# Windowed attention ahead of two MLPs: old and new scores merged by mask into 128 columns before the exponential

## The chip, the cores and the metric

One core of one Trainium2 chip. The metric is device time in microseconds (us), the median of three runs. Engines: PE multiplies matrices (PEld loads its stationary side), DVE is VectorE, ACT is ScalarE, POOL is GpSimd, SP issues most DMAs.

## What is computed

Attention over `q`, `k`, `v` of shape (2, 8, 768, 64) (batch, heads, positions, width), in which a position sees itself, the 127 positions before it, and the first four positions (the sinks); then two MLPs over the 1536 tokens of 512, of width 2048:

```
scores = scale * q @ k^T
keep = (pos_k < 4) | ((rel >= 0) & (rel < 128))          # rel = pos_q - pos_k
a = softmax(where(keep, scores, -1e9));  x = a @ v
x -> (x @ w_in), g = h if h >= 1, 0 if h <= -1, else (h + 1)^2 / 4;  x = g @ w_out
x -> (x @ w2_in), g = h if h > 0, else exp(h) - 1;                   out = g @ w2_out
```

All is float32; the weights arrive as 64-bit numbers and are converted on the chip.

## The kernel before

*Attention* (class `Attn`). 768 positions are six blocks of 128. A segment is two blocks of one batch: six segments. A job is one pair of heads of a segment, four jobs a segment, 24 in all. A job goes through these steps:

- **T** (`st_T`, line 456): k and q are transposed on PE (line 466, four transposes) and copied to `qkT` (line 470, on DVE in the front, on ACT later). POOL keeps the last block of k for the next segment and copies the four sink keys behind each block (lines 474 to 481).
- **S0, S1** (`st_S`, line 484), one for each block: for each of the two heads one matmul (line 506) of 128 queries against 260 columns: 128 old keys (the block before), 4 sinks, 128 new keys. The first block of a batch has no old keys and 132 columns. DVE adds the mask, scales and takes the maximum (line 510), ACT takes the exponential and its sum (line 512), POOL copies the sink columns (line 515).
- **X** (`st_X`, line 531): the probabilities are transposed on PE (line 539), 128 columns at a time: two for a block with old keys, so eight for a job, six in the first segment of a batch; ACT copies them to `pt` (line 541), one copy for each head.
- **V** (`st_V`, line 544): v times `pt` (line 564), the two heads in two 64-column halves of the array; DVE copies the result to `xb` (line 567).
- After four jobs the **sink stage** (`st_sink`, line 569) adds the sinks' part, divides by the sums and writes the token tiles `xh`, `xl` for the MLPs. `vsink` (line 353) sets up the sink values; `load_vsink` (line 345) loads them by two DMAs from ACT's queue.

*The MLPs* (class `Moe`). 96 items: two MLPs, three token tiles of 512, 16 pieces of the width. An item is 12 matmuls of 512 columns in `gemm1` (line 171) and 12 in `gemm2` (line 210), which runs two items later; each product is made of three matmuls on split numbers. The weights of an MLP are converted once, with its first token tile (lines 138 to 145, ACT and DVE), and split for each item (`wsplit`, line 158 on ACT, line 160 on DVE in the first 16 items and on POOL later).

*Order.* `stages` (line 403) is a generator which gives one step at a time; `ahead` (line 415) and `FIRST` say how far T, S0 and S1 of a job run ahead of its V. The first two segments run before the MLPs (lines 764 to 774), with PE's order as it is written; the accumulator banks that the MLPs do not yet need serve as spares (`spare`), eight in all. Then `between` (line 779) draws steps from the generator at each of the four stops of an item, with `PULLS` steps for each stop: 1.0 in the first token tile, 0.8 in the second; there the attention has two banks. The DMAs of the front are issued in program order (lines 764 to 770, and `load` in `stages`).

## Time and profile before

| | us |
|---|---|
| median of three runs | 661.48 (661.33 to 661.95) |
| the profiled execution | 662.93 |
| its span, first to last instruction | 661.2 |
| PE busy | 638.8 (97%) |
| ACT busy | 450.6 (68%) |
| DVE busy | 376.2 (57%) |
| POOL busy | 267.8 (40%) |

The span lies inside the execution's time; 1.7 us lie around it. Shares over the whole span hide that the kernel has parts with different limits: the first product matmul (line 171) starts at 58.0 us, the attention is over before 266.5 us, and the rest is products. So the rows are cut by these times, and the first part of the products once more at 152.8 us, where the conversion of the first weights ends. Busy time of an engine is the time in which at least one of its instructions ran; neighbouring instructions overlap a little, so that means of single instructions add up to more than that. An entry "x4" counts records; a matmul on float32 leaves two records, a transpose one.

### The profile page before, as it was taken

What the parts mean: (1) busy time and instruction counts of PE and PEld (TensorE: products, weight loads), DVE (VectorE), ACT (ScalarE), POOL (GpSimd) and SP (SyncE); (2) the same over time, 40 slices, a digit from 0 to 9 for tenths busy, and PEclk for the clock granted to TensorE, in tenths of its full rate; (3) what the DMA queues carried; (4) which work ended last, traced back from release to release, by engine and by line L of the source; (5) the groups of instructions that cost most, each with busy time, mean ns of one, the idle gap of its engine ahead of it and who ended that gap; (6) DMA issues with size and microseconds to landing.
All of it is one profiled execution on the core that took longest, in us unless ns stands there. A gap on an engine that the chain in (4) does not pass through costs nothing.

```text
span 661.2 us, 9257 instructions
## 1 busy us (share of the span) xinstructions
PE 638.8 (97%) x3090; PEld 500.5 (76%) x3090; DVE 376.2 (57%) x742; ACT 450.6 (68%) x913; POOL 267.8 (40%) x310
## 2 busy tenths in 40 slices
PE   5899999999999999999999999999999999999995
PEld 2666767766777767888878888888888888888884
DVE  2899989999435244224987878777432222322221
ACT  2998998997666666557768878776655555555542
POOL 4320113112125334443645655554544444444441
PEclk8998999999999999999999999999999999999999
DMA  6577454764200000000433332321010000100001
GB/s 172 126 186 203 126 170 135 207 198 143 56 13 13 13 0 1 1 0 1 159 118 105 99 105 90 109 93 50 0 64 1 0 1 0 64 0 1 1 0 69
DMA packets 66922, 47.91 MB, mean 72 GB/s; under 512 B 44848, under 2 KB 61232, under 8 KB 66864
## 3 DMA queue, kind: packets, MB, share of 16 engines
q1 hardware_dynamic: 65552, 46.94, 24.6%
q8 instruction: 26, 0.43, 0.3%
q10 hardware_dynamic: 1312, 0.28, 0.2%
q14 instruction: 32, 0.26, 0.1%
HBM read 44.06 MB, written 3.15 MB: 71 GB/s over the span
## 4 chain that ended last, share of the span: by engine, by line
PE 81%; DVE 7%; issue 4%; ACT 4%; DMA 2%; POOL 1%; POOLq 0%; SPq 0%; DVEq 0%; ACTq 0%
PE h L171 36%; PE y L210 35%; PE S L506 4%; PE ops L564 3%; PE tps L539 2%; DVE ca L143 2%; PE qkps L466 1%; DVE F L145 1%; DVE ca L142 1%; DVE wl L160 1%; ACT pt L541 1%; DMA st<-in_moe_w_in_dram 1%; DVE P L510 1%; ACT P L512 1%; PE y L267 1%
## 5 line engine op out<-in xcount | busy, mean ns | idle before, releaser
L160 POOL TENSOR_TENSOR wl<-F,wh 128x512 fp32r<-128x512 f32 x160 | 219.6, 1380 | 229.6 <-ACT wh L158 216.9
L158 ACT CAST wh<-F 128x512 fp32r<-128x512 f32 x192 | 117.5, 618 | 97.1 <-PE h L171 89.4
L171 PE MATMUL h<-xh,wh 128*128 128x512 f32 x384 | 154.3, 402 | 0.5 <-DVE g L180 0.5
L171 PE MATMUL h<-xh,wl 128*128 128x512 f32 x384 | 150.5, 392 | 0.0
L171 PE MATMUL h<-xl,wh 128*128 128x512 f32 x384 | 150.5, 392 | 0.0
L187 ACT CAST gh<-g 128x512 fp32r<-128x512 f32 x96 | 59.7, 621 | 62.1 <-DVE g L184 36.2
L188 DVE TENSOR_TENSOR gl<-g,gh 128x512 fp32r<-128x512 f32 x96 | 68.3, 712 | 49.0 <-ACT gh L187 48.7
L184 DVE SCALAR_TENSOR_TENSOR g<-g,h 128x512 f32<-128x512 f32 x48 | 33.0, 687 | 110.9 <-ACT g L183 110.9
L171 PEld LDWEIGHTS h<-xh,wh 128*128 128x128 f32 x384 | 72.4, 189 | 20.6 <-issue 5.3
L171 PEld LDWEIGHTS h<-xh,wl 128*128 128x128 f32 x384 | 72.3, 188 | 15.3
L171 PEld LDWEIGHTS h<-xl,wh 128*128 128x128 f32 x384 | 72.7, 189 | 14.2 <-DVE xl L608 0.4
L210 PE MATMUL y<-gh,wh 128*128 128x512 f32 x192 | 78.4, 408 | 0.0
L210 PE MATMUL y<-gh,wl 128*128 128x512 f32 x192 | 75.2, 391 | 0.0
L210 PE MATMUL y<-gl,wh 128*128 128x512 f32 x192 | 74.9, 390 | 0.0
L145 DVE CUSTOM_DVE_ANT_0 F<-ca,F 128x1024 uint16<-128x1024 uint16 x64 | 71.5, 1119 | 4.5 <-DVE ca L143 1.8
L210 PE MATMUL y<-wh,gh 128*128 128x512 f32 x184 | 71.6, 389 | 0.0
L210 PE MATMUL y<-wl,gh 128*128 128x512 f32 x184 | 71.6, 389 | 0.0
L210 PE MATMUL y<-wh,gl 128*128 128x512 f32 x184 | 71.6, 389 | 0.0
L180 DVE SCALAR_TENSOR_TENSOR g<-h,g 128x512 f32<-128x512 f32 x48 | 33.0, 687 | 45.2 <-ACT g L179 45.1
L512 ACT ACTIVATE P<-P,nb 128x260 f32<-128x260 f32 (+1 forms) x96 | 46.6, 491 | 15.5 <-DVE nb L510 13.4
L515 POOL COPY psn<-P 128x8 f32<-128x8 f32 x48 | 13.0, 271 | 89.8 <-ACT P L512 81.9
L510 DVE CUSTOM_DVE_ANT_0 P<-S,mask 128x260 f32<-128x260 f32 (+1 forms) x96 | 34.8, 401 | 24.1 <-PE S L506 23.5
(105 smaller groups left out, 912.3 us busy)
## 6 DMA issues: line engine op xcount, KB each, us to landing
st<-in_moe_w_in_dram SPq DMA_DIRECT2D x32, 512.0 KB, 3.9
st<-in_moe_w_out_dram SPq DMA_DIRECT2D x32, 512.0 KB, 3.8
kn<-in_k_dram SPq DMA_DIRECT2D x48, 64.0 KB, 2.3
vn<-in_v_dram SPq DMA_DIRECT2D x32, 96.0 KB, 2.4
out_dram<-o SPq DMA_DIRECT2D x12, 256.0 KB, 2.1
qn<-in_q_dram SPq DMA_DIRECT2D x44, 64.0 KB, 2.4
vn<-in_v_dram SPq DMA_DIRECT2D x16, 64.0 KB, 2.1
qn<-in_q_dram ACTq DMA_DIRECT2D x4, 64.0 KB, 3.0
```

The lines of the kernel that those rows point to most:

```text
L145: nc.vector.tensor_tensor(out=r, in0=ai, in1=r, op=ALU.add)
L158: nc.scalar.copy(hi, src)
L160: (nc.vector if i < self.KF else nc.gpsimd).tensor_tensor(out=lo, in0=src, in1=f32(hi), op=ALU.subtract)
L171: nc.tensor.matmul(h, lhsT=w[:, k * 128:(k + 1) * 128], rhs=x[:, k, c0:c0 + n], start=(k == 0 and p == 0), stop=(k == self.KD - 1 and p == 2))
L180: nc.vector.scalar_tensor_tensor(out=g, in0=h, scalar=1.0, in1=g, op0=ALU.max, op1=ALU.min)
L184: nc.vector.scalar_tensor_tensor(out=g, in0=g, scalar=-1.0, in1=h, op0=ALU.add, op1=ALU.max)
L187: ac = nc.scalar.copy(gh, g)
L188: dv = nc.vector.tensor_tensor(out=gl, in0=g, in1=f32(gh), op=ALU.subtract)
L210: nc.tensor.matmul(self.y[c], lhsT=a, rhs=b, start=(first and p == 0), stop=(last and p == 2))
L506: nc.tensor.matmul(S[h], lhsT=qT[hs, n, :], rhs=kT[hs].rearrange("p j k -> p (j k)")[:, j0 * KW:j0 * KW + W], start=True, stop=True)
L510: dv = nc.vector.tensor_tensor_reduce(out=o, in0=S[h], in1=self.mask[ty], op0=ALU.add, op1=ALU.min, scale=-self.scale, scalar=3.0e38, accu ...
L512: ac = nc.scalar.activation(o, o, AF.Exp, bias=nb[:, n, h:h + 1], scale=-1.0, accum_out=sm[:, n, 2 * pr + h:2 * pr + h + 1])
```

## The change

- Of each block's 128 columns, a query needs either the old or the new key: column c is new for queries from c on, and old for those before. The scores of a block are made in 64x64 tiles, in such places that for half of the columns the wanted score is where it should be; where a 64x64 square holds both kinds, DVE copies one over the other by a mask (`copy_predicated`, two for a head). So 128 columns and 4 sinks are left for the maximum and the exponential, instead of 260 columns.
- S0 and S1 become one step S, with both blocks of a pair in one bank for each head.
- X transposes four tiles instead of eight and ACT makes one copy; POOL separates old and new by two `affine_select` of 512 elements.
- The copy to `qkT` is on ACT throughout, and that to `xb` too.
- Order: V of a job is drawn one job later, T, S and V have new places, `PULLS` is (0.7, 0.7, 1.0), `FIRST` 8; loads of k and q run four jobs ahead instead of three; in the front POOL too follows the written order.
- The sink values' selectors (`sink_sets`) are made ahead of the front; the rest of `vsink` stays in the first sink stage; `load_vsink` is issued on SP, after the loads of v of job 0.

```diff
-PULLS = (1.0, 0.8, 1.0)
+PULLS = (0.7, 0.7, 1.0)
 LAG = 2
-FIRST = 9
+FIRST = 8
 NSINK = 4
 BLK = 128
 KW = BLK + NSINK
-WP = KW + BLK
+HB = BLK // 2
+BW = KW + HB + NSINK
...
-        self.ld_p = pool("ld", 3)
+        self.ld_p = pool("ld", 4)
+        self.v_p = pool("v", 3)
         self.qk_p = pool("qk", 2)
-        self.p_p = pool("p", 4)
+        self.p_p = pool("p", 3)
...
+        pick = const.tile([128, HB], F32, tag="pickf", name="pickf")
+        nc.gpsimd.memset(pick, 1.0)
+        for c, op, sg in ((0, ALU.is_ge, 1), (1, ALU.is_gt, -1)):
+            r = pick[c * HB:(c + 1) * HB]
+            nc.gpsimd.affine_select(out=r, in_=r, pattern=[[-sg, HB]], compare_op=op, fill=0.0, base=0, channel_multiplier=sg)
...
-            self.nc.scalar.dma_start(out=raw[:, 0, :], in_=self.v[b, :, 0:NSINK, :])
+            self.nc.sync.dma_start(out=raw[:, 0, :], in_=self.v[b, :, 0:NSINK, :])
...
+    def sink_sets(self):
...
-        ahead = (("T", 2), ("S0", 1), ("X", 0), ("S1", 1), ("V", 0))
-        todo = {p: [] for p in range(-2, len(jobs))}
+        ahead = (("S", 1), ("T", 2), ("V", -1), ("X", 0))
+        todo = {p: [] for p in range(-3, len(jobs) + 1)}
         for j in range(len(jobs)):
             for i, (what, d) in enumerate(ahead):
-                todo[max(j - d - (j < FIRST and d > 0), -2)].append((j, i, what))
-        sink = None
-        for p in range(-2, len(jobs)):
-
-            order = "XT01V".index if self.spare else "T0X1V".index
-            for j, _, what in sorted(todo[p], key=lambda x: (order(x[2][-1]), x[0])):
+                todo[max(j - d - (j < FIRST and d > 0), -3)].append((j, i, what))
+        sink, ready = {}, []
+        for p in range(-3, len(jobs) + 1):
+
+            order = ("XTVS" if p < FIRST else "VXTS").index if self.spare else "STVX".index
+            for j, _, what in sorted(todo[p], key=lambda x: (order(x[2]), x[0])):
                 seg, pr = jobs[j]
                 st = state[seg]
-                if what == "V" and sink:
-                    yield from sink[0]
-                    yield sink[1]
-                    sink = None
                 if what == "T":
                     self.st_T(seg, pr, st)
-                    load("k", j + 3)
-                    load("q", j + 3)
-                elif what == "S0":
-                    self.st_S(seg, pr, st, 0)
-                elif what == "S1":
-                    self.st_S(seg, pr, st, 1)
+                    load("k", j + 4)
+                    load("q", j + 4)
+                elif what == "S":
+                    self.st_S(seg, pr, st)
+                    ready.append((seg, pr, st))
                 elif what == "X":
                     self.st_X(seg, pr, st)
+                    while ready:
+                        self.sums(*ready.pop(0))
                 else:
                     self.st_V(seg, pr, st)
                     load("v", j + 2)
                 yield None
-            if p >= 0 and jobs[p][1] == np_ - 1:
+                if what == "V" and pr == np_ - 1:
+                    yield from sink[seg]
+                    yield seg
+            if 0 <= p < len(jobs) and jobs[p][1] == np_ - 1:
                 seg = jobs[p][0]
-                sink = self.st_sink(seg, state[seg]), seg
-                if self.spare and p + 1 < len(jobs):
-
-                    yield next(sink[0])
-                else:
-                    yield from sink[0]
-                    yield seg
-                    sink = None
+                sink[seg] = self.st_sink(seg, state[seg])
+                yield next(sink[seg])
 
...
-        late = self.spare and (seg, pr) not in self.jobs[:2]
-        (nc.vector.tensor_copy if late else nc.scalar.copy)(T[:, 1:, 0:BLK], bank)
+        nc.scalar.copy(T[:, 1:, 0:BLK], bank)
...
+    def st_S(self, seg, pr, st):
+
         nc, D, nq = self.nc, self.D, self.nq
         b, q0 = seg[0], seg[1]
+        qT, T = st["qk", pr]
+        Tk = T.rearrange("p j k -> p (j k)")
+        if "sm" not in st:
+            st["sm"] = self.s_p.tile([128, nq, self.H], F32, tag="sm", name="sm")
+            st["ps"] = self.s_p.tile([128, nq, self.H * (NSINK + 2)], F32, tag="psn", name="psn")
+        nb = self.s_p.tile([128, nq, 2], F32, tag="nb", name="nb")
+        P = st["P", pr] = self.p_p.tile([128, nq, 2, KW], F32, tag="P", name="P")
+        S = [self.bank([128, 512], "S") for _ in range(2)]
+        lead = HB + NSINK
+        for n in range(nq):
+            u = lead + n * BW
+            for h in range(2):
+                hs = slice(h * D, (h + 1) * D)
+                for c in range(2):
+                    o, r = (u - c * lead, n * KW + c * HB) if q0 + n else (u, KW)
+                    N = (KW + (HB, lead)[c]) if q0 + n else KW
+                    nc.tensor.matmul(S[h][c * HB:(c + 1) * HB, o:o + N], lhsT=qT[hs, n, c * HB:(c + 1) * HB],
+                                     rhs=Tk[hs, r:r + N], start=True, stop=True, skip_group_check=True)
+        n0 = 0 if q0 else 1
         for h in range(2):
+            a = S[h][:, lead:lead + nq * BW].rearrange("p (n c) -> p n c", c=BW)
+            lo = S[h][:, 0:nq * BW].rearrange("p (n c) -> p n c", c=BW)
+            for c, to, data in ((0, a[:, :, 0:HB], a[:, :, KW:KW + HB]), (1, a[:, :, HB:BLK], lo[:, :, 0:HB])):
+                r = slice(c * HB, (c + 1) * HB)
+                nc.vector.copy_predicated(to[r, n0:], self.pick[r].unsqueeze(1).to_broadcast([HB, nq - n0, HB]), data[r, n0:])
+            for n in range(nq):
+                o = P[:, n, h, :]
+                dv = nc.vector.tensor_tensor_reduce(out=o, in0=a[:, n, 0:KW], in1=self.mask[min(q0 + n, 2)], op0=ALU.add, op1=ALU.min,
+                                                    scale=-self.scale, scalar=3.0e38, accum_out=nb[:, n, h:h + 1])
+                ac = nc.scalar.activation(o, o, AF.Exp, bias=nb[:, n, h:h + 1], scale=-1.0,
+                                          accum_out=st["sm"][:, n, 2 * pr + h:2 * pr + h + 1])
...
+    def sums(self, seg, pr, st):
+        nc = self.nc
+        P = st["P", pr]
+        sinks = st["ps"][:, :, 2 * pr * NSINK:2 * (pr + 1) * NSINK]
+        nc.gpsimd.tensor_copy(sinks.rearrange("p n (h s) -> p n h s", h=2), P[:, :, :, BLK:KW])
+    def st_X(self, seg, pr, st):
+        nc, nq = self.nc, self.nq
+        P = st["P", pr]
+        bank = self.bank([128, 2 * nq, 128], "tps")
         for h in range(2):
+            for n in range(nq):
+                nc.tensor.transpose(bank[:, h * nq + n, :], P[:, n, h, 0:BLK], self.idn)
+        t = st["pt", pr] = self.pt_p.tile([128, 4 * nq, 128], F32, tag="pt", name="pt")
+        t2 = t.rearrange("p (a two) q -> p a two q", two=2)
+        old, new = t2[:, :, 0, :], t2[:, :, 1, :]
+        nc.scalar.copy(new, bank)
+        for o, op, sg in ((old, ALU.is_gt, 1), (new, ALU.is_ge, -1)):
+            nc.gpsimd.affine_select(out=o, in_=new, pattern=[[0, 2 * nq], [-sg, 128]], compare_op=op, fill=0.0, base=0,
+                                    channel_multiplier=sg)
...
+        nc.scalar.copy(st["xb"][:, pr, :], bank)
 
...
-        for what, j in (("k", 1), ("k", 2), ("q", 2), ("v", 0)):
+        for what, j in (("k", 1), ("k", 2), ("q", 2), ("k", 3), ("q", 3), ("v", 0)):
             attn.load(what, *attn.jobs[j])
-        with tc.manual_schedule(engines={mybir.EngineType.PE}):
-            go(n=1)
+        attn.load_vsink()
+        attn.sink_sets()
+        with tc.manual_schedule(engines={mybir.EngineType.PE, mybir.EngineType.Pool}):
             moe.load(1)
             attn.load("v", *attn.jobs[1])
             moe.load(3)
-            go(n=19)
-        flag = windowed(tc, const, prm)
-        with tc.manual_schedule(engines={mybir.EngineType.PE}):
+            go(n=18)
+            flag = windowed(tc, const, prm)
             go(upto=need[0])
```

## Rows read from the trace of the kernel before

**Rows 1.** Stretch, length, busy PE, PEld, DVE, ACT, POOL, granted clock, DMA share, GB/s.

```profile
18.00:58.00 40.00, 35.21 (x281) 25.64 (x279) 36.81 (x129) 39.17 (x118) 9.99 (x42) 1.00 0.66 164
58.00:152.80 94.80, 93.82 (x478) 67.66 (x478) 87.52 (x203) 86.12 (x192) 15.90 (x38) 0.98 0.60 173
152.80:266.50 113.70, 112.53 (x600) 82.88 (x599) 55.45 (x130) 74.73 (x166) 41.67 (x53) 1.00 0.10 26
266.50:649.60 383.10, 382.61 (x1687) 315.98 (x1685) 188.89 (x249) 244.69 (x426) 190.82 (x139) 1.00 0.14 46
```

**Rows 2.** Chain of waits, 58 to 190 us: start us, length us, what.

```profile
166.95 0.44 PE qkps L466 x4
167.39 1.40 PE y L210 x6
168.78 0.64 PE S L506 x4
169.42 1.59 PE y L210 x6
171.01 0.87 PE tps L539 x8
...
175.49 1.02 PE ops L564 x12
```

**Rows 3.** The same chain over the whole span, where products run alone.

```profile
280.25 2.72 PE y L210 x12
```

**Rows 4.** Timeline, 5 to 15.5 us: start, length, engine, line, operation [idle <-releaser].

```profile
5.40 2.05 ACTq L350 DMA_DIRECT2D vraw<-in_v_dram  x2
...
7.49 1.28 ACT L741 ACT_TABLE_LOAD   x1 [7.49 <-DMA qn<-in_q_dram]
...
11.64 0.61 POOL L368 CAST one<-oneh 112x512 fp32r<-112x512 f32 x1
...
12.57 1.03 POOL L385 TENSOR_TENSOR vs<-vpart,sel 96x512 fp32r<-96x512 f32 x1
13.03 0.96 SPq L398 DMA_DIRECT2D kn<-in_k_dram  x2
...
13.79 1.68 PE L506 MATMUL S<-qkT 64*128 64x132 f32 x8 [6.36 <-POOL qkT L481]
...
14.97 0.41 ACT L512 ACTIVATE P<-P,nb 128x132 f32<-128x132 f32 x1 [5.03 <-DVE nb L510]
```

**Rows 5.** Groups by line and shape, whole span: busy us, mean ns | idle before.

```profile
L512 ACT ACTIVATE P<-P,nb 128x260 f32<-128x260 f32 x80 | 40.3, 509 | 9.6 <-DVE nb L510 7.5 <-POOL qkT L481 1.6
...
L510 DVE CUSTOM_DVE_ANT_0 P<-S,mask 128x260 f32<-128x260 f32 x80 | 30.9, 423 | 17.1 <-PE S L506 16.6 <-POOL qkT L481 0.3
...
L541 ACT COPY pt<-tps 128x512 f32<-128x512 f32 x32 | 17.4, 579 | 2.5 <-PE tps L539 2.4
...
L567 DVE COPY xb<-ops 128x256 f32<-128x256 f32 x24 | 10.1, 420 | 12.3 <-PE ops L564 12.1
...
L512 ACT ACTIVATE P<-P,nb 128x132 f32<-128x132 f32 x16 | 6.3, 399 | 5.9 <-DVE nb L510 5.8
...
L510 DVE CUSTOM_DVE_ANT_0 P<-S,mask 128x132 f32<-128x132 f32 x16 | 4.0, 289 | 7.1 <-PE S L506 6.9
...
L332 DVE SCALAR_TENSOR_TENSOR mask<-rel,prm,mask 128x128 f32<-128x128 f32 x2 | 0.7, 344 | 0.0
...
L340 DVE COPY mask<-mask 128x128 f32<-128x128 f32 x1 | 0.2, 218 | 0.0
```

**Rows 6.** Timeline, 53 to 59 us.

```profile
54.13 0.52 ACT L512 ACTIVATE P<-P,nb 128x260 f32<-128x260 f32 x1
...
55.13 0.51 ACT L512 ACTIVATE P<-P,nb 128x260 f32<-128x260 f32 x1
```

**Rows 7.** Line 145 by stretch: minimum/median/maximum ns, first and last start.

```profile
L145 DVE CUSTOM_DVE_ANT_0 F<-ca,F x26: 675/686/1357, 57.4 to 149.8; 128x1024 uint16<-128x1024 uint16 x26
...
L145 DVE CUSTOM_DVE_ANT_0 F<-ca,F x30: 682/1622/1705, 314.0 to 454.9; 128x1024 uint16<-128x1024 uint16 x30
```

More of the change, by code (lines that the diff above doesn't have):

```diff
@@ new lines, in masks @@
+        self.pick = const.tile([128, HB], I32, tag="pick", name="pick")
+        nc.gpsimd.tensor_copy(self.pick, pick)
+        nc.vector.tensor_scalar(out=neg, in0=rel, scalar1=0.0, scalar2=None, op0=ALU.is_lt)
+        nc.vector.scalar_tensor_tensor(out=ring, in0=neg, scalar=float(BLK), in1=rel, op0=ALU.mult, op1=ALU.add)
+        nc.vector.scalar_tensor_tensor(out=far, in0=neg, scalar=1.0e6, in1=rel, op0=ALU.mult, op1=ALU.add)
+        m0, m1, m2 = self.mask = [const.tile([128, KW], F32, tag=f"mask{ty}", name=f"mask{ty}") for ty in range(3)]
@@ L351, in load_vsink @@
             self.vraw.append(raw)
+    def sink_sets(self):
+        nc, const, H, D = self.nc, self.const, self.H, self.D
+        R = H * NSINK
+        L = 3 * R + 2 * H
+        self.one = const.tile([L, H, D], F32R, tag="one", name="one")
+        one = const.tile([L, H], F32, tag="oneh", name="oneh")
+        nc.gpsimd.memset(one, 0.0)
+        for j in range(2):
+            nc.gpsimd.affine_select(out=one[3 * R:], in_=one[3 * R:], pattern=[[-1, H]],
+                                    compare_op=ALU.not_equal, fill=1.0, base=-j * H, channel_multiplier=1)
+        nc.gpsimd.tensor_copy(self.one, one.unsqueeze(2).to_broadcast([L, H, D]))
+        self.sel = const.tile([3 * R, H], F32, tag="sel", name="sel")
+        nc.gpsimd.memset(self.sel, 1.0)
+        for g in range(3):
+            s = self.sel[g * R:(g + 1) * R]
+            nc.gpsimd.affine_select(out=s, in_=s, pattern=[[-NSINK, H]], compare_op=ALU.is_ge, fill=0.0,
+                                    base=0, channel_multiplier=1)
+            nc.gpsimd.affine_select(out=s, in_=s, pattern=[[NSINK, H]], compare_op=ALU.is_ge, fill=0.0,
+                                    base=NSINK - 1, channel_multiplier=-1)
@@ L481, in st_T @@
         nc.gpsimd.tensor_copy(kT[:, :, BLK:], self.sk[pr].to_broadcast([128, nq + lead, NSINK]))
[L482 to L484 removed]
+        if q0 + nq < self.S // BLK:
+            nc.gpsimd.tensor_copy(self.kept[pr], T[:, nq, 0:BLK])
+        st["qk", pr] = qT, T
+    def st_S(self, seg, pr, st):
         nc, D, nq = self.nc, self.D, self.nq
         b, q0 = seg[0], seg[1]
[L487 to L517 removed]
@@ L519, in chunks @@
-    def chunks(self, q0):
-        out = []
-        for n in range(self.nq):
-            qb = q0 + n
-            if qb == 0:
-                out.append((n, 0, 0))
-            else:
-                out.append((n, 0, qb - 1))
-                out.append((n, KW, qb))
-        return out
-    def st_X(self, seg, pr, st):
-        nc, D, nq = self.nc, self.D, self.nq
-        b, q0 = seg[0], seg[1]
-        P = st.pop(("P", pr))[0]
-        ch = self.chunks(q0)
-        for h in range(2):
-            bank = self.bank([128, len(ch), 128], "tps")
-            for i, (n, o, kb) in enumerate(ch):
-                nc.tensor.transpose(bank[:, i, :], P[n][:, h, o:o + 128], self.idn)
-            t = self.pt_p.tile([128, len(ch), 128], F32, tag="pt", name="pt")
-            nc.scalar.copy(t, bank)
-            st["pt", pr, h] = t
+        qT, T = st["qk", pr]
@@ L548, in st_V @@
         vn = self.nat.pop(("v", seg, pr))
-        ch = self.chunks(q0)
-        runs = []
-        for i, (n, o, kb) in enumerate(ch):
-            if runs and runs[-1][0] == kb:
-                runs[-1][2] += 1
-            else:
-                runs.append([kb, i, 1])
+        first = 1 if q0 == 0 else 0
+        runs = [(q0 - 1, 0, 1)] * (1 - first) + [(q0 + n, 2 * n + 1, 2 if n + 1 < nq else 1) for n in range(nq)]
         if "xb" not in st:
```

115 lines of the change are left out of this document (32 added, 83 removed).

## Prediction

> **What bounds the kernel now.** I read the busy time by stretch first [rows 1]. From 266.5 us on, PE is busy for 382.61 of 383.10 us with the two products alone: no attention is left there, so the change can gain nothing in it. From 58.0 to 266.5 the products and attention share PE, which is full in both stretches (93.82 of 94.8 us, 112.53 of 113.7). In the first of them DVE (87.52 us) and ACT (86.12 us) are nearly full as well, because the weights are converted there; in the second they have room. Before 58.0 it is another matter: from 18 to 58 us ACT is busy 39.17 of 40 us, DVE 36.81, PE 35.21. So the front is bound by ACT, with DVE close behind, and the middle by PE.
>
> Next the chain of waits in a steady piece of the middle [rows 2]. It gives the price of an attention step on PE: its own piece, plus what the six product matmuls behind it take above 1.36 us, their pace when nothing lies between (2.72 for twelve, [rows 3]). A T costs 0.44 + 0.03 = 0.47 us, an S step of one block 0.64 + 0.23 = 0.87, an X of eight transposes 0.87 + 0.03 = 0.90, a V 1.02 + 0.23 = 1.25. A job (one pair of heads, two blocks) has two S steps: 4.36 us. By the order that the code yields, 22 groups of twelve product matmuls and about 7.3 jobs lie in the first stretch of the middle, and some 15 jobs in all after 58 us; 15 x 4.36 = 65 us agrees with what is left of 208.5 us after 50 groups x 2.72 = 136 us (72.5, with four sink stages and small waits in it).
>
> Last the start of the front [rows 4]. PE's first scores wait until 13.79 us, 6.36 us of it for POOL, which copies the sink keys into qkT only behind the set-up of the sink values (up to the 1.03 us product at 12.57). That set-up waited for the vraw DMAs, whose issue holds ACT's queue for 2.05 us from 5.40, so that ACT's table load stands at 7.49 and its first exponential at 14.97.
>
> **The change, part by part.** *Scores.* The steps S0 and S1 become one. A transpose's piece (four of 128 columns in 0.44 us, [rows 2]) gives 0.11 us for 128 columns in one pass; a step's four records (two heads, two passes, 260 columns) would take 0.89 us one after another and take 0.64 with their entry, so two row halves already run side by side; V's twelve records (16 units of 128 columns, 1.76 us in a row) take 1.02, so two column halves do too. Four 64x64 tiles at once are in no row. If both kinds compose, a block costs two passes of 200 columns = 0.34 us instead of 0.45, and entering and leaving (0.87 - 0.45 = 0.42) is paid once for two blocks: 0.42 + 0.69 = 1.11 us instead of 1.74, a gain of 0.63. If the column halves queue, it is 0.42 + 1.38 = 1.80, a loss of 0.06. I take the first, as V's row shows the column side at the same width of 64.
>
> *Transposes.* Four instead of eight (six in the first segment of a batch): 0.45 us off, or 0.22. V keeps its columns.
>
> *PE in the middle.* 15 jobs x 0.63 = 9.4; 11 x 0.45 + 4 x 0.22 = 5.8; together 15.2 us. The new order leaves one S, one T and one X more to the middle (scores of jobs 0 to 8 in front instead of 0 to 9): 1.11 + 0.47 + 0.45 = 2.0 back. Left: 13 us.
>
> *DVE in the middle.* A job's four evacuations go from 260 to 132 columns, 423 to 289 ns [rows 5]: -0.54 us; the xb copy (420 ns) goes to ACT; four predicated copies of 64 partitions x 128 elements come. The trace has none. Below, the plain 128-element copy (218 ns); above, the dearest 128-element instruction (344 ns); I take 0.29, the row for 132 columns read from PSUM with a second operand. Net +0.2 us a job. But the pulls fall from 1.0 to 0.7 a call, with 20 steps in a segment instead of 24: 6.2 jobs instead of 7.3 lie in the first stretch, so DVE there stays near 86 us of work while PE's falls from 94 to about 84. DVE takes over as the bound of that stretch, and two nearly full engines wait for each other. In addition both banks go to one S step, and the T behind it waits until DVE has emptied the first (two copies, two evacuations: about 1.1 us, against 1.4 us of products in between). For all this I take 3 us off, bounds 0 and 7. PE in the middle: -10 us, between -6 and -13.
>
> *POOL.* Two selects of 512 elements a job: between 0.61 (the cast of 512 elements) and 1.03 us each (the product of two tensors, [rows 4]), so 1.2 to 2.1 us a job, against about 3 us a job of ACT in front. V is moved a job behind X, so this is hidden; if POOL's hand-written order fails to keep up, V waits, and that is in the rivals.
>
> *Front, start.* The sink values' set-up moves to the first sink stage; only the selectors, which wait for nothing, stay ahead. The vraw DMAs go to SP. The first scores then wait for ACT's copy of qkT: about 2 us earlier without the DMA issues, then a few tenths of POOL's sink copies. First exponential near 9.7 instead of 14.97: -5 us, -4 if ACT gains nothing. SP pays: k and q of job 4 are issued behind four more DMAs and 1.5 MB of weights, at 0.48 us apiece [rows 4], and land near 18 us, some 1.5 us after ACT wants them.
>
> *Front, ACT's work.* The first and the third exponential of a job start 1.00 us apart, accumulators included [rows 6]; at 132 columns they are 110 ns shorter [rows 5], so 0.39 each instead of 0.50. One pt copy of two falls away (579 ns in its row; with the overlap of 0.1 that neighbours on ACT show, an estimate of 0.48; 0.38 for the three-chunk copies of a first segment), one T copy of the same size comes from DVE, and an xb copy of half of it (estimate 0.30). Front, before: scores 10 x 2.0, pt 10 x 0.48 + 8 x 0.38, T 3 x 0.48 = 29.3. After: 9 x 1.56 + 8 x 0.48 + 10 x 0.48 + 8 x 0.30 = 25.1. So -4 us. At the end the last V now stands behind a select and nothing of X or S is left to fill ACT: +1.5.
>
> *Sum.* Front -5 + 1.5 - 4 + 1.5 = -6 (between -2 and -10); middle -10; the stretch after 266.5 unchanged. -16 us on a span of 661.2, or of 662.93 for the profiled execution with what lies around it: 646.9. The median of the runs, 661.48, lies 1.45 below that execution, so I predict 645.5.
>
> **The rivals.**
> A, *DVE sets the middle.* With conversions, 128-column selects and bank waits the first stretch hardly shrinks (94.8 to about 93), and the gain of the middle is 5: 651. For it: 87.52 of 94.8 us [rows 1], and a conversion instruction of DVE which takes 686 ns there but 1622 where POOL splits weights all the time [rows 7]; 12 selects that each held one up by 0.65 would add 8 us to DVE. Against it: POOL is busy only 15.90 us in that stretch now. The Trainium skill's "TensorEngine Tiling (Array Packing)", section PSUM Bottleneck, says that tiling speeds TensorE but not the emptying of PSUM, which may become the bound; by that rule A is the outcome, 651, and the trace bears it out for that stretch alone. "SBUF — State Buffer" of the Trainium skill, section Who interferes with whom, says that DVE and GpSimd share one port pair as an exclusive lock; rows 7 agree for this instruction.
>
> B, *the four tiles don't run side by side.* The scores' gain of 9.4 us becomes a loss of 0.9; partly hidden where DVE binds: 655.
>
> C, *slower: two banks and one DVE queue.* PE takes its instructions in order. If DVE reaches the score evacuations only behind a whole conversion and a split (four instructions of up to 0.69 us, the length of L145 in [rows 7]; an estimate of 2.5), a bank comes free 2.5 + 1.1 us after the scores, against 1.4 to 2.8 us of products; T and the next S then each stand for about a microsecond. Ten jobs in the converting stretch x 2 us = 20, against 16 + 3 gained: 662.5. It decides from 1.8 us a job. Against it: V, X and T need only one bank each now.
>
> D, *the front gains all of its 10 us and nothing waits in the middle*: 638.
>
> **How the numbers follow.** Forecast 0.64 (639 to 652), A 0.15, B 0.06, C 0.09, D 0.06. A difference under 0.2% (1.3 us) can't be told from no change here. Faster: forecast, A, B, D and little of C = 0.89; slower 0.07; same 0.04. The range must take in D's edge and A and B: 637 to 656; C is left out.
>
> **What would show it.** Right: the first L171 matmul near 52 us instead of 58; the first exponential near 10; S as one piece of about 0.9 us with eight records a block starting together; tps pieces of 0.44 us; product groups at 1.36 to 1.6 us with attention over before 262 us. A would show as DVE busy over 95% up to the last conversion, with PE waiting for it; B as S pieces of 1.6 us; C as PE waits on the mask evacuation ahead of T and S of over 1 us each. I would be wrong in the front if a late k or q, or POOL's selects ahead of V, stop ACT there.

## The result: slower, and where the time went

The changed kernel takes 668.36 us (median; 667.26 to 669.76) where the kernel before takes 661.5: ratio 1.0104, 95% interval 1.0084 to 1.0123. The forecast was 645.5, the range 637 to 656. The traces are of single executions, 668.36 us after and 662.93 before; their spans are 666.2 and 661.2 us.

The stretches of [rows 1], now of the kernel after (same columns):

```profile
18.00:58.00 40.00, 28.62 (x257) 19.67 (x258) 30.62 (x114) 29.58 (x91) 21.67 (x47) 0.85 0.66 165
58.00:152.80 94.80, 88.07 (x503) 63.80 (x500) 89.61 (x213) 81.26 (x187) 25.86 (x42) 0.98 0.54 153
152.80:266.50 113.70, 110.59 (x660) 82.15 (x659) 63.58 (x170) 76.23 (x183) 53.84 (x68) 1.00 0.18 49
266.50:649.60 383.10, 382.86 (x1671) 310.26 (x1670) 190.46 (x251) 243.08 (x426) 191.50 (x141) 1.00 0.15 46
```

Three things are to be seen. In the front no engine is full any more: ACT fell from 39.17 to 29.58 of 40 us, PE from 35.21 to 28.62, and PE's granted clock is 0.85. In the second row PE has lost work (93.82 to 88.07) and DVE is now the fuller engine. In the last row PE is as full as before but has done 1671 matmuls instead of 1687.

That last row is the surprise. The chain of waits between 400 and 420 us, where products run alone (start, length, what):

```profile
404.51 2.80 PE h L172 x12
407.31 2.74 PE y L211 x12
410.05 2.80 PE h L172 x12
412.85 2.74 PE y L211 x12
```

Before, twelve matmuls of either product took 2.72 us. [rows 3] shows it for y; the chain of the kernel before between 400 and 420 us shows it for h:

```profile
409.12 2.72 PE h L171 x12
```

The same instructions at the same granted clock of 1.00 now take 2.80 and 2.74: one item (twelve h, twelve y) 5.54 us instead of 5.44, one h matmul 233.3 ns instead of 226.7.

Landmarks read from PE's own records (starts of matmuls; an item is 24 product matmuls, 96 items in all):

| | before | after |
|---|---|---|
| first product | 58.0 | 59.4 |
| item 16 | 189.4 | 183.2 |
| item 32 | 299.1 | 298.6 |
| last matmul | 654.6 | 659.9 |

The front lost 1.4 us (forecast: a gain of 6), items 0 to 31 gained 1.9 (forecast 10, and some of that is eaten by the slower pace), and 64 items without any attention lost 5.9 (forecast 0). Together +5.3, from starts that are not rounded.

The front's start went nearly as forecast. PE's timeline of the kernel after (start, length, instruction, idle time before it):

```profile
8.30 0.79 PE L509 MATMUL S<-qkT 64*64 64x132 f32 x16 [0.77 <-POOL qkT L484]
...
21.23 0.66 PE L472 MATMUL qkps<-idn,kn 128*128 128x128 f32 x2 [6.84 <-DMA kn<-in_k_dram]
...
23.75 1.39 PE L509 MATMUL S<-qkT 64*64 64x132 f32 x16
...
27.62 0.91 PE L509 MATMUL S<-qkT 64*64 64x196 f32 x16
```

ACT's first exponential, from the same stretch:

```profile
10.39 0.41 ACT L522 ACTIVATE P<-P,nb 128x132 f32<-128x132 f32 x1
```

Scores start at 8.30 instead of 13.79 and the first exponential at 10.39 instead of 14.97 [rows 4]. Then PE stands for 6.84 us for k of job 4. SP's queue in the same stretch shows what stood ahead of it:

```profile
12.08 0.44 SPq L107 DMA_DIRECT2D st<-in_moe_w_in_dram  x1
12.57 1.01 SPq L403 DMA_DIRECT2D vn<-in_v_dram  x2
13.63 0.47 SPq L110 DMA_DIRECT2D st<-in_moe_w_out_dram  x1
14.14 0.43 SPq L107 DMA_DIRECT2D st<-in_moe_w_in_dram  x1
14.70 0.94 SPq L410 DMA_DIRECT2D kn<-in_k_dram  x2
```

The k load was issued right behind three weight loads of 512 KB each, and from 14 to 22 us the DMA engines are busy 0.99 of the time, at 272 GB/s. In the kernel before the same three loads were issued from 8.37 to 12.51 us, while PE stood 6.36 us for POOL [rows 4], and its trace has no wait of PE for a load between 8 us and the first product.

### The profile page after: what moved, and what is told of

Same layout as the page of the kernel before. It is cut to its first block, busy times and chain, and to the rows that moved or that the text cites. A ratio compares the mean times of both kernels' runs of the same rounds, so it can differ in the third digit from the quotient of the medians.

```text
span 666.2 us, 9583 instructions
## 1 busy us (share of the span) xinstructions
PE 631.7 (95%) x3202; PEld 489.3 (73%) x3202; DVE 386.8 (58%) x805; ACT 444.2 (67%) x922; POOL 303.7 (46%) x337
## 4 chain that ended last, share of the span: by engine, by line
PE 75%; DVE 8%; ACT 6%; DMA 4%; issue 3%; POOL 1%; SPq 1%; POOLq 0%; ACTq 0%; DVEq 0%
PE h L172 34%; PE y L211 33%; PE ops L565 2%; PE S L509 2%; DMA st<-in_moe_w_in_dram 2%; DVE ca L144 2%; DVE F L146 2%; ACT P L522 1%; PE qkps L472 1%; PE tps L541 1%; ACT F L140 1%; ACT ca L139 1%; DMA kn<-in_k_dram 1%; DVE ca L143 1%; PE y L268 1%
## 5 line engine op out<-in xcount | busy, mean ns | idle before, releaser
L172 PE MATMUL h<-xl,wh 128*128 128x512 f32 x384 | 152.3, 397 | 0.9 <-POOL xl L609 0.9
L189 DVE TENSOR_TENSOR gl<-g,gh 128x512 fp32r<-128x512 f32 x96 | 72.7, 758 | 51.5 <-ACT gh L188 51.1
L146 DVE CUSTOM_DVE_ANT_0 F<-ca,F 128x1024 uint16<-128x1024 uint16 x64 | 74.3, 1164 | 4.3 <-DVE ca L144 1.8
L547 POOL TENSOR_SCALAR_AFFINE_SELECT pt<-pt 128x512 f32<-128x512 f32 x48 | 35.7, 744 | 32.5 <-ACT pt L545 30.9
L139 ACT ACTIVATE ca<-st 128x512 f32<-128x512 f32 x64 | 43.1, 674 | 7.4 <-DVE F L146 3.4
L144 DVE SCALAR_TENSOR_TENSOR ca<-st,ca 128x512 int32<-128x512 int32 x64 | 47.3, 742 | 1.1
```

The source lines that it names most:

```text
L139: nc.scalar.activation(a, w1.bitcast(F32), AF.Copy, scale=2.0 ** -112)
L144: nc.vector.scalar_tensor_tensor(out=ai, in0=w1, scalar=-0x80000000, in1=ai, op0=ALU.bitwise_and, op1=ALU.bitwise_or)
L146: nc.vector.tensor_tensor(out=r, in0=ai, in1=r, op=ALU.add)
L172: nc.tensor.matmul(h, lhsT=w[:, k * 128:(k + 1) * 128], rhs=x[:, k, c0:c0 + n], start=(k == 0 and p == 0), stop=(k == self.KD - 1 and p == 2))
L189: dv = nc.vector.tensor_tensor(out=gl, in0=g, in1=f32(gh), op=ALU.subtract)
L547: nc.gpsimd.affine_select(out=o, in_=new, pattern=[[0, 2 * nq], [-sg, 128]], compare_op=op, fill=0.0, base=0, channel_multiplier=sg)
```

## Experiments: the products' pace

The same program text computes the products in both kernels. What differs is where their tiles stand in SBUF: the change alters the sizes of the attention tiles, and the x tiles and MLP tiles (weights, split weights, g) are allocated around them. Before, x begins at byte 27040 of a partition and the split weights (wh0) at 192672; after, at 26528 and 196320. The experiments move tiles and touch nothing else. Edits are on the kernel named first.

**e1, before, x and MLP tiles where after has them.**

```
-            raw = self.const.tile([R, 1, self.D], F32, tag=f"vraw{b}", ...)
+            raw = self.vr_p.tile([R, 1, self.D], F32, tag=f"vraw{b}", ...)
+        self.vr_p = pool("vr", 1)      # behind a_s
+        self.pad = pool("pad", 1).tile([128, 912], F32, tag="pad", name="pad")
```

> The kernel before, with the token tiles and all tiles of the MLPs at the very SBUF addresses that they have in the changed kernel (x 512 bytes lower, the MLP's tiles 3648 bytes higher); no instruction differs. Theory P (the changed kernel's slower products, 5.54 us an item instead of 5.44, come from where the tiles lie): the items of the last stretch go to 5.54 us, and the time rises by 96 x 0.10 = about 9.5 us, to 671. Theory Q (they come from something else in the change): 661.5, items at 5.44.

668.30 us, ratio 1.0105 (1.0088 to 1.0122), an item 5.54 us: the kernel before, with nothing but addresses changed, is as slow as the kernel after. Theory P's pace came, its 671 did not: the 64 items of pure products got 5.9 us longer, items 0 to 31 no longer (240.4 us, before 241.1).

**e2 and e3, one group of tiles each**: only the vr_p line (x 512 bytes lower), or only the pad (MLP tiles 3648 bytes higher).

> The kernel before, with the token tiles alone 512 bytes lower, where the changed kernel has them; MLP tiles as before. If the place of the moving token tiles is what matters: gemm1's matmuls at 233 ns, gemm2's at 227, some 7.5 us more (669). If the place of the MLP tiles is what matters: 661.5.

> The kernel before, with the MLP's tiles alone 3648 bytes higher, where the changed kernel has them; token tiles as before. If the place of the weights and of g matters: gemm1 and gemm2 both slower, 668 to 671. If the token tiles' place matters: 661.5 to 663.

e2: 661.45, 5.44 us an item. e3: 669.09, ratio 1.0124 (1.0104 to 1.0144), 5.54. So it is the MLP tiles' place, and the next three ask how finely it counts, and whether against x.

**e5, e6, e7: 64 bytes.** A tile of [128, 16] float32 ahead of the MLP tiles (e5 in after, e6 in before), or ahead of x, so that all move (e7, in before).

> The kernel after with one unused tile of 64 bytes a partition behind the attention pools, so that every MLP tile stands 64 bytes higher: at 32 modulo 128, as in the kernel before (before: 110752 and so on, 160 modulo 2048; after: 114400, 1760 modulo 2048, which is 96 modulo 128); nothing else is changed. Theory P1 (the products' pace hangs on where the MLP tiles stand within 128 bytes): an item of pure products falls from 5.54 to 5.44 us, the time from 668.4 to 661 (659 to 663). Theory P2 (it hangs on the place within a larger unit, or on how high the tiles stand): 5.54 us and 668 as after.

> The kernel before with the same 64-byte tile: MLP tiles at 96 modulo 128, everything else where it was. P1: an item of pure products goes from 5.44 to 5.54 us, 661.5 to 668.5 (667 to 670). P2: 5.44 us and 661.5.

> The kernel before with a 64-byte tile ahead of the x tiles, so that x, the attention tiles and the MLP tiles all stand 64 bytes higher, at 96 modulo 128 (x at 27104). P1 with the place itself counting: 5.54 us an item and 668.5. P1 with the place of the weights against x counting (both were at 32 modulo 128 before; here both are at 96): h matmuls at 226.7 ns as before, and 661.5 to 663 in all. P2: 661.5.

e5: 667.10, 5.53 us an item, a miss for P1; its chain of waits:

```profile
403.69 2.79 PE h L172 x12
406.49 2.73 PE y L211 x12
```

e6: 669.45, ratio 1.0115 (1.0098 to 1.0132), 5.54: 64 bytes cost 7.5 us. e7: 662.03, 5.44: the same 64 bytes cost nothing when x moves along. The chain of waits of e6:

```profile
408.65 2.74 PE y L210 x12
411.39 2.80 PE h L171 x12
```

And that of e7:

```profile
407.96 2.72 PE h L171 x12
410.68 2.72 PE y L210 x12
```

The distance between x, which the h matmul streams, and wh0, which it loads as weights, orders all these runs:

| kernel | x | wh0 | distance | remainder to 256 | item, us |
|---|---|---|---|---|---|
| before | 27040 | 192672 | 165632 | 0 | 5.44 |
| e2 | 26528 | 192672 | 166144 | 0 | 5.44 |
| e7 | 27104 | 192736 | 165632 | 0 | 5.44 |
| e6 | 27040 | 192736 | 165696 | 64 | 5.54 |
| e3 | 27040 | 196320 | 169280 | 64 | 5.54 |
| after, e1 | 26528 | 196320 | 169792 | 64 | 5.54 |
| e5 | 26528 | 196384 | 169856 | 128 | 5.53 |

The MLP tiles moved as one group in every run, so the table alone does not tell the weights from the other MLP tiles, which ACT, DVE and POOL read and write meanwhile. The trace of the kernel after narrows it. From 320 to 655 us it has 30 places where an h matmul follows another while ACT, DVE and POOL all stand (in 29 of them no DMA moves bytes either), and each of these steps takes 233 ns, like the others. One of them lies between the end of a POOL instruction (560.51 + 1.29) and the start of one on ACT (562.29):

```profile
560.51 1.29 POOL L161 TENSOR_TENSOR wl<-F,wh 128x512 fp32r<-128x512 f32 x1 [1.76 <-ACT wh L159]
561.80 0.39 PE L172 MATMUL h<-xl,wh 128*128 128x512 f32 x1
562.04 0.39 PE L172 MATMUL h<-xh,wl 128*128 128x512 f32 x1
562.29 0.62 ACT L159 CAST wh<-F 128x512 fp32r<-128x512 f32 x1 [1.86 <-PE h L172]
```

So the slower pace needs no other engine at work. What h itself reads in SBUF is x and the split weights.

**e9, the test of that rule on the kernel after**: the two 16-byte nb tiles (64 bytes with their alignment) go ahead of x, so that the distance becomes 169728, which leaves nothing over 256.

```
+    Attn.nb_p = ctx.enter_context(tc.tile_pool(name="nb", bufs=2))   # ahead of xp
-        nb = self.s_p.tile([128, nq, 2], F32, tag="nb", name="nb")
+        nb = self.nb_p.tile([128, nq, 2], F32, tag="nb", name="nb")
```

> The kernel after with the two 16-byte nb tiles ahead of the x tiles instead of behind the other attention tiles: x stands 64 bytes higher, the MLP tiles stay where the kernel after has them, and the distance from x to the split weights is 169728 bytes instead of 169792. Theory R (the distance from the moving x tile to the split weights decides: no remainder to 256 bytes in the three kernels with 5.44 us an item, 64 or 128 in the five with 5.53 to 5.54): an item of pure products takes 5.44 us, the time falls from 668.4 by 7 to 9 us to 660 (659 to 661.5), so the kernel after is faster than before by 0 to 0.4%. Rival H (how high the tiles stand, or the place of x alone): 5.54 us and 668.

660.52 us, ratio 1.0005 (0.9981 to 1.0029). Its chain:

```profile
408.68 2.72 PE y L211 x12
411.40 2.72 PE h L172 x12
```

The pace is back, 7.8 us with it, and what is left of the change is a difference from before that can't be told from none. Against the kernel before, e9's first product is 0.6 us later, and items 0 to 31 take 237.4 us instead of 241.1; the profiled execution (659.52) is one of the shortest of e9's ten (659.46 to 667.04).

## Experiments: the front

Five kernels, all made from after with its slow pace, move the three weight loads or free POOL's order.

**e4 and e11, the loads later in SP's queue.** In after, the front begins with load(1), v of job 1, load(3), and then 18 steps.

```
e4:   +go(n=2)   moe.load(1)   attn.load("v", ...)   moe.load(3)   go(n=16)
e11:   attn.load("v", ...)   go(n=6)   moe.load(1)   go(n=4)   moe.load(3)   go(n=8)
```

> The changed kernel with two steps (T of jobs 0 and 1) drawn ahead of the first three weight loads, so that k and q of jobs 4 and 5 are issued before 1.5 MB of weights. Theory L (the front lost its gain because k of job 4 lands only at 21.1 us): PE's wait of 6.8 us for it shrinks to under 2, the first product comes at 55 us instead of 59.4, and the time falls by about 4 us, to 664. Theory M (the front is bound by the order of POOL and the waits between engines): the load comes earlier, but the first product stays within 1 us of 59.4.

> The kernel after with v of job 1 issued first, and the three first weight loads (1.5 MB) behind the sixth and the tenth step of the front instead of ahead of the first. Theory D: without these 1.5 MB at 12 to 22 us the k, q and v loads land when they are wanted, PE's waits for DMA in the front (6.8 for k, 1.6 for v) go, and the first product comes at 53 to 56 us, the time at 662 to 665. Rival L (a chain of latencies through PE, DVE, ACT and POOL sets the pace once the loads are there): first product at 58 to 60, 667 to 669.

e4: 667.15, first product at 59.9: theory M's outcome, since PE waits for k of job 4 no more and for no other load by more than 1.6 us (v), and still the products begin no earlier. e11: 667.49, first product at 60.0: rival L's outcome, though here a load is late again, v instead of k. SP's queue in e11:

```profile
25.37 0.47 SPq L110 DMA_DIRECT2D st<-in_moe_w_out_dram  x1
25.88 0.43 SPq L107 DMA_DIRECT2D st<-in_moe_w_in_dram  x1
26.36 1.37 SPq L403 DMA_DIRECT2D vn<-in_v_dram  x2
```

And PE's timeline in e11:

```profile
31.73 1.75 PE L565 MATMUL ops<-pt,vn 128*64 128x256 f32 x8 [6.24 <-DMA vn<-in_v_dram]
```

In after and in e11 the wait of 6 to 7 us hits the load that is issued right behind the weights. e4 shows that this wait is not what the front's length hangs on alone. One term that the waits do not show is PE's clock: the granted clock from 18 to 58 us is 1.00 in before [rows 1], 0.85 in after, 0.81 in e11 and 0.74 in e4 (before has its low stretch earlier, 0.50 from 12 to 18 us). In e4 PE was busy for 4.24 of the 8 us from 14 to 22 us; then the granted clock is 0.50, the level of 1.2 GHz, from 22 to 30 us. It is low again from 39 to 46 us (0.53), and a step S takes 1.61 us there, one of the same size behind it 0.91:

```profile
41.17 1.61 PE L509 MATMUL S<-qkT 64*64 64x196 f32 x16
45.64 0.91 PE L509 MATMUL S<-qkT 64*64 64x196 f32 x16
```

How much of the front the clock costs, against the engines' waits for each other, no run separates.

**e13, the loads on ACT's queue; e16, behind steps 14 and 16.**

```
e13:  +eng = nc.scalar if self.n_ld <= 3 else nc.sync      # in Moe.load, for both DMAs
e16:   attn.load("v", ...)   go(n=14)   moe.load(1)   go(n=2)   moe.load(3)   go(n=2)
```

> The kernel after with the three first weight loads (1.5 MB) issued from ACT's queue instead of SP's, at the same point of the program. Theory W (the 1.5 MB stand ahead of k of job 4 in SP's queue, and the wait goes with them): PE's wait for k, 6.8 us in the kernel after, falls under 2, no other load is waited for by more than 1 us, and the first product comes at 54 to 57 us: 663 to 666. Rival L (a chain of latencies sets the pace of the front): k's wait falls too, but the first product stays at 58.5 to 60 and the time at 667 to 669. Rival B (the transfers share the same 16 engines, so k is as late from a second queue): k's wait stays at 5 to 7 us.

> The kernel after with the three first weight loads behind the fourteenth and the sixteenth step of the front. Theory W: k and v of jobs 1 to 6 land when they are wanted, PE waits for no load by more than 2 us before the weights go out, and what the weights cost is paid at the front's end, where the first product waits for their conversion: first product at 55 to 58. Rival L: no load is waited for, and the first product comes at 58.5 to 60 all the same, since PE, DVE, ACT and POOL wait for each other.

e13: 665.72. No k is waited for, but ACT's copy of qkT now waits behind the weight loads on its own queue, and PE for what hangs on it, right at the start (waits of e13 from 8 to 60 us: total, times, longest):

```profile
PE S L510 <- POOL qkT L485: 5.7, 1, 5.7
...
ACT qkT L476 <- DMA st<-in_moe_w_out_dram: 5.2, 1, 5.2
```

So the first product still stands at 58.8, which is rival L's, and the total, which is theory W's, fell by 2.6 us mostly in the items behind it. e16: 664.61, ratio 1.0049 (1.0032 to 1.0065), first product 56.8, inside theory W's 55 to 58; PE still waits 3.2 us for two v loads. W holds as far as these 2.6 us. For the other 5 us that were forecast there is no test, only candidates in the trace of the kernel after: PE waits for exponentials (3.9 us in four places after 43 us), for the sink values that POOL builds (1.8), for v (1.6), and behind the 6.84 us in which it stood, part of its time lies at the lower clock level (1.2 GHz; the granted clock is 0.71 on the mean of 22 to 30 us): the S step at 23.75 us takes 1.39, the larger one at 27.62 only 0.91 (first fence of PE, above).

**e10, POOL's order left to the scheduler** (Pool out of the engines whose order is written by hand).

> The kernel after with POOL's order in the front left to the scheduler, as its other engines' are, instead of the written order. Theory L (the front waits for POOL's instructions in their written order: selects, sink copies, the sink values): the first product comes 2 to 5 us earlier than 59.4, the time falls from 668.4 to 664 to 666. Rival D (late DMAs hold the front, whatever POOL's order): first product at 59 to 60, 668.

665.95, but the first product comes at 59.2: theory L missed, and the 2.4 us came off items 0 to 31 (236.3 us against 239.2). With the fast place (e15, e18 below) the same edit gave -0.8 and +1.2 us, so nothing is to be had from it that holds.

## Experiments: the middle

In the kernel after PE waits 7.8 us in all ahead of the T transposes (sum of the gaps between the last product matmul and the first qkps matmul, less the pace of one matmul); before, 0.07. One of the longest, on DVE's timeline of the kernel after:

```profile
132.41 0.22 DVE L517 COPY_PREDICATED S<-pick,S 64x64 f32<-64x64 int32 x1
132.55 0.68 DVE L144 SCALAR_TENSOR_TENSOR ca<-st,ca 128x512 int32<-128x512 int32 x1
133.16 0.68 DVE L189 TENSOR_TENSOR gl<-g,gh 128x512 fp32r<-128x512 f32 x1
133.76 0.68 DVE L146 CUSTOM_DVE_ANT_0 F<-ca,F 128x1024 uint16<-128x1024 uint16 x1
134.46 0.49 DVE L517 COPY_PREDICATED S<-pick,S 64x64 f32<-64x64 int32 x2
134.87 0.28 DVE L520 CUSTOM_DVE_ANT_0 P<-S,mask 128x132 f32<-128x132 f32 x1
...
135.08 0.28 DVE L520 CUSTOM_DVE_ANT_0 P<-S,mask 128x132 f32<-128x132 f32 x1
```

And on PE's:

```profile
135.48 0.41 PE L472 MATMUL qkps<-idn,kn 128*128 128x128 f32 x2 [2.02 <-issue]
```

The trace names no releaser for it ("issue"), but T starts its weights at 135.44, right when the second evacuation (135.08 + 0.28) has emptied the first bank. Between the first predicated copy and the second, DVE does three instructions of the conversion and the products, 1.9 us: this is rival C's mechanism.

**e8, one more empty step between S and T** in the middle (an extra yield, pulls 0.84 instead of 0.7).

> The kernel after with one more empty step between a job's S and the T behind it, in the middle only (24 steps a segment instead of 20, so the pulls are 0.84 a call instead of 0.7: jobs follow each other as before). Theory C (T stands for a bank because both are in S): PE's wait ahead of the T transposes falls from 7.8 us to under 2, the wait of other steps stays, and the time falls by 4 to 6 us, from 668.4 to 663.5. Rival C' (what is late is DVE's whole queue, so the wait only moves to another step): T's wait falls, that of S, X or V rises by as much, 667 to 669.

668.56: the wait ahead of T fell to 2.7, but the S pieces grew by 2.6 us in sum, the gaps ahead of the sink transposes by 3.6, and the items 0 to 31 took 239.2 us as in the kernel after. C' holds in that the wait moves; that it is DVE's queue which moves it is its reading, and the next two runs ask for that.

**e12 and e14, one conversion instruction of DVE less** (the shift of ca by 3 bits left out, so the converted weights are wrong), in after and in before. A shift is 0.42 us, not the 0.69 that e12's expectation says, and the 3.8 us in e14's is 3.3.

> The kernel after without the shift of ca by 3 bits on DVE in the conversion of the weights (its values are then wrong; one DVE instruction of 128x512 less for each of 32 conversions, some 0.69 us each in the first stretch of the middle). Theory Q (in that stretch DVE is the bound, and T waits because DVE's queue is late): PE's waits ahead of T, now 7.8 us, fall under 3 and the stretch gets 5 to 8 us shorter: 661 to 663. Rival S (T waits for the two score evacuations themselves, whatever else DVE has): the waits stay at 6 to 8 us and the time at 666 to 668.

> The kernel before without the shift of ca by 3 bits on DVE in the conversion of the weights (its values are then wrong); 418 ns each (the row L142), 32 times. In the kernel after the same cut gave 2.3 us in the front and 3.8 us in the first sixteen items (123.8 to 120.5 us), though T went on waiting. Theory Q (DVE binds the first stretch of after, PE that of before): the first sixteen items of before take 131.4 us now and 130.5 to 131.5 without the shift; the time falls by 0 to 1.5 us plus what the front gains. Rival Q' (DVE held both kernels there alike): 126 to 128 us for the sixteen items, and the time falls by 4 to 6 us.

e12: 663.48, 4.9 us less than after. In its profiled execution (661.24, the shortest of ten) the front is 2.3 us shorter and the first sixteen items 3.3 (123.9 to 120.6). T's wait stayed at 7.4, where rival S had it, and neither theory's time came: Q missed with T's wait and with 661 to 663, S with 666 to 668. e14: 663.10, ratio 1.0021 (1.0012 to 1.0031), so slower than before, if by little; the front was 2.7 us longer, which nothing here explains, and the sixteen items took 130.3 instead of 131.4, near theory Q's 130.5 to 131.5 and far from Q' (126 to 128). The chain of waits from 60 to 180 us, as shares by line, first of the kernel before:

```profile
by line: PE h L171 25.3%; PE y L210 21.2%; PE S L506 9.4%; PE ops L564 7.0%; PE tps L539 4.7%; issue 4.0%; DVE wl L160 4.0%; DMA st<-in_moe_w_in_dram 4.0%; DMA st<-in_moe_w_out_dram 3.3%; DVE ca L143 3.2%; PE qkps L466 2.3%; DVE F L145 1.8%
```

The same of the kernel after:

```profile
by line: PE h L172 15.4%; DMA st<-in_moe_w_in_dram 9.9%; PE y L211 9.7%; DVE F L146 6.8%; issue 6.5%; DVE ca L144 5.2%; ACT F L140 4.5%; ACT P L522 4.4%; DVE wl L161 3.6%; ACT ca L139 3.6%; DMA st<-in_moe_w_out_dram 3.1%; ACT g L179 2.9%; P
```

And of e12:

```profile
by line: PE h L171 32.3%; PE y L210 31.0%; PE S L508 5.6%; issue 5.6%; PE ops L564 5.2%; DMA st<-in_moe_w_out_dram 3.6%; PE qkps L471 3.5%; PE tps L540 2.2%; DVE ca L143 1.7%; DVE P L519 1.2%; DVE S L516 1.1%; DVE gl L188 1.1%; POOL xl L608
```

Before, PE's own lines lead the chain. After, the products hold 25% of it, and the conversion of the weights (its DMA, ACT's ca and F, DVE's ca and F) about 33%. Without the shift the products hold 63%. So the bound of this stretch moved from PE towards the conversion, as rival A says: the same cut is worth 3.3 us in after and 1.2 in before. But the shifts are 9.3 us of DVE's time from 60 to 150 us, so DVE is not alone in binding it, and T's wait did not fall with DVE's load.

Nor did DVE's load fall with the change. Its conversion instruction got longer, first before, then after, from 60 to 150 us:

```profile
L145 DVE CUSTOM_DVE_ANT_0 F<-ca,F 128x1024 uint16<-128x1024 uint16 x25 | 17.8, 716 | 0.3
L146 DVE CUSTOM_DVE_ANT_0 F<-ca,F 128x1024 uint16<-128x1024 uint16 x22 | 17.7, 812 | 0.0
```

With its other conversions and splits this comes to some 4 us. Rival A expected it, with 8 us, from POOL's selects; POOL is busy for 25.86 us in the stretch instead of 15.90, but that the selects are the cause no run shows.

## Experiments: put together

**e15**: e9 with POOL's order free. **e17**: e9 with e16's order of loads. **e18**: all three.

> The kernel after with x 64 bytes higher (the two nb tiles ahead of it) and with POOL's order in the front left to the scheduler. Each alone gave -7.8 us (660.5) and -2.4 us (665.95) against 668.36. If they add up: 658 (657 to 659.5), 0.5% below the kernel before; if POOL's order only gave back what the place gives too: 660 to 661.

> The kernel after with x 64 bytes higher (the two nb tiles ahead of it) and the three first weight loads behind the fourteenth and the sixteenth step of the front. Alone they gave -7.8 us (660.52) and -3.8 us (664.61) against 668.36. If the causes are separate they add up: 656.8 (656 to 658), 0.7% below the kernel before. If the front's gain is swallowed by the middle once the products are at 5.44 us (DVE binds there): 659 to 660.5.

> The same with POOL's order in the front left to the scheduler too. If POOL's written order holds the front beside the loads: 655 to 656.5. If POOL's order only mattered while k was late: as the run without it, 656.5 to 658.

e15: 659.73, ratio 0.9976 (0.9963 to 0.9990). e17: 658.37, ratio 0.9943 (0.9930 to 0.9957): faster than both kernels, 3.8 us below before, though 1.6 above the sum of the parts. e18: 659.59, ratio 0.9966 (0.9953 to 0.9978). e15 and e17 lie between their two theories, e18 outside both of its own. Its first product is the earliest of the three, 56.2, and its items 0 to 31 take 239.8 us against 236.1 in e17: what the front gains, the middle gives back. The stretch 58 to 152.8 us of e17, then of e18 (columns of [rows 1]):

```profile
58.00:152.80 94.80, 89.39 (x514) 65.24 (x515) 92.11 (x217) 84.48 (x192) 29.04 (x43) 1.00 0.56 162
58.00:152.80 94.80, 87.53 (x498) 64.13 (x500) 89.96 (x213) 82.01 (x187) 26.36 (x40) 0.98 0.55 157
```

DVE is busy for 97% of it in e17 and for 95% in e18, so a fuller DVE is not why e18's middle is longer. Its granted clock is 0.98: 3.4 us from 135.3 us on lie at the lower level, which by an estimate (half the pace for that long) makes at most 1.7 of the 3.7 us. The rest is open. Over the four kernels with the fast place (e9, e15, e17, e18) items 0 to 31 take 235.4 to 239.8 us, so one trace gives the middle's gain to some 2 us only.

## Why the prediction was wrong, step by step

*The stretch after 266.5 unchanged: wrong, and this decided the sign.* The step took the products' pace (2.72 us, [rows 3]) as a property of the instructions, and put the change's effect on it at nothing. e1, e3, e6 and e9 show that the pace hangs on the tiles' place; the change moved the tiles, and twelve h take 2.80 us. Worth 7.8 us (after against e9).

*The front, -6: wrong in size by 7.* The start's -5 came as -4.6 (first exponential), with the scores 5.5 us earlier. "Late k and q +1.5" failed: PE stood 6.84. The step had seen the 1.5 MB in SP's queue and charged 0.48 us for each issue, but not the time in which the transfers themselves fill all DMA engines. The prediction named a late k as what could break the front; it should have priced it. But that is not all: e4 takes this wait away and the first product comes no earlier (59.9), and the best order of loads (e16) brings the first product 2.6 us forward. The other step that failed is "ACT's work, -4": the work did fall, but ACT was no longer the bound (29.58 of 40 us busy), so it shortened nothing. What holds the front instead, the clock among it, stays open for some 5 us.

*The middle, -10: right in PE's own work, wrong in the waits; -3.7 in size* (e9 against before, both at 5.44 us an item; -1.3 to -5.7 with e15, e17 and e18). By the gaps between PE's records:

| term | forecast | measured |
|---|---|---|
| scores, with one S more | -8.3 | -9.0 |
| transposes, with one X more | -5.4 | -6.3 |
| T, one more | +0.5 | +0.6 |
| V | 0 | +2.1 |
| waits | +3 (0 to 7) | +8.3 ahead of T, +0.6 elsewhere |

The four 64x64 tiles do run side by side: the eight score matmuls of 196 and 200 columns (sixteen records) take 0.91 us in the timeline (27.62 us, above), about the forecast's piece of 0.9, and B is out. The V term was forgotten: V was moved a job behind X, so one V more than before lies in the middle (about 1.2 us); the other 0.9 is dearer V steps. The waits are above their upper bound. A and C, held for rivals of each other, came together: DVE is nearly full in the converting stretch, and PE stands where both banks are in the scores. That the second follows from the first is not shown, as T's wait stayed in e12. The Trainium skill's "TensorEngine Tiling (Array Packing)", section PSUM Bottleneck, which stood beside A, says that the emptying of PSUM may become the bound once tiling speeds TensorE. The trace agrees in the engine alone: DVE is busy 89.61 of 94.8 us, PE 88.07, but from 60 to 150 us the scores' merging and emptying (L517, L520) are 16.1 us of DVE's work and the conversion and splits of the weights 59.5.

*Prices of single instructions.* From the groups by line and shape of the kernel after (busy us, mean ns):

```profile
L517 DVE COPY_PREDICATED S<-pick,S 64x128 f32<-64x128 int32 x64 | 18.2, 296 | 7.1 <-PE S L509 5.5
...
L547 POOL TENSOR_SCALAR_AFFINE_SELECT pt<-pt 128x512 f32<-128x512 f32 x48 | 35.7, 744 | 32.5 <-ACT pt L545 30.9
...
L522 ACT ACTIVATE P<-P,nb 128x132 f32<-128x132 f32 x96 | 37.8, 396 | 11.1 <-DVE nb L520 10.9
```

Taken were 290 ns, 610 to 1030 and 399: on the mean none of these failed.

So the sum of -16 became +5.4 in the profiled executions by +7.7 for the pace (5.9 after item 32, 1.8 before it), +7.4 for the front and +6.3 for the middle; by the medians it is +6.9, since the execution of the kernel before that was profiled is a long one. What stays open: what holds the front where no load is late, why PE waits ahead of T, why e17 falls 1.6 us short of the sum of its parts, and the pace's rule beyond the distances that were run.

## What to carry to other kernels

An edit that changes the size of any tile moves all tiles allocated behind it; before a stage is put down as unchanged, compare the time of one repeated group of its instructions in both traces, and if it differs, the addresses. A large load costs the queue its transfer beside its issue (0.44 us to issue and 6.84 us of waiting here): look who is issued behind it, and whether that one is wanted before the bytes are through. Then test by moving it, since the wait that goes may uncover others: e4 lost the wait, and its products began no earlier. And before work taken off the fullest engine is counted as time, see how full the next one is in that stretch: here DVE was at 87.52 of 94.8 us, and PE's wait ahead of T went from 0.07 to 7.8 us.

## What the runs showed of the hardware

The matmul of 128x128 weights against 512 columns takes 226.7 ns at a granted clock of 1.00 in the runs whose distance in SBUF between the streamed tile and the weights leaves nothing over 256 bytes, and 233.3 ns in those where it leaves 64 (twelve take 2.79 us in e5, where it leaves 128). Moving one group of tiles by 64 bytes is worth 7.5 us of 662 (e6), and moving both by the same 64 nothing (e7). The distances of all fast kernels (before, e2, e7, e9) leave 256 over 512; a distance that is a multiple of 512, or one that leaves 192 over 256, was not tried, and what in the chip causes it no run shows. The y matmuls, whose operands both lie among the MLP tiles and moved together, slowed only from 226.7 to 228.3 ns.
